# First batch's local probabilities turned on TensorE into strips of 64 keys

## The chip, the cores and the metric

One program runs on one core of a Trainium2 chip. The metric is the device time of one execution in microseconds; the kernel before takes 929.92 us (median of 3 runs, 927.62 to 931.52). Engines are named as in the profile: PE is TensorE, DVE VectorE, ACT ScalarE, POOL GpSimd, SP SyncE, which issues most DMAs.

## The reference

Attention over 8 batches, 8 heads, 576 positions, 64 dimensions, then a gated feed-forward network (FFN) over the 4608 tokens. Heads 0 to 3 see the last 32 positions ("local"), heads 4 to 7 every 32nd position ("strided"):

```python
rel = pos[:, None] - pos[None, :]
mask_local = (rel >= 0) & (rel < 32)
mask_strided = (rel >= 0) & (pos[None, :] % 32 == pos[:, None] % 32)
scores = np.where(masks, scale * q @ k.T, -1e9)
attn = softmax(scores)
x = (attn @ v).transpose(0, 2, 1, 3).reshape(4608, 512)
h = x @ w_in                      # 512 to 2048
g = h * clip(h + 3, 0, 6) / 6
out = g @ w_out                   # 2048 to 512
```

All data are fp32.

## The kernel before

**Work.** Heads go in pairs; a pair gives one chunk c of x, 128 features (two heads by 64) by 576 tokens. Chunks 0 and 1 are local, 2 and 3 strided. The first batch takes them in the order 0, 2, 1, 3 (`TURNS`). The FFN takes 512 tokens of a batch at a time, and the 64 left over of each batch are gathered and done four batches together. The FFN's operands are split into a high and a low fp32r part, so that each product is three matmuls: first product `ph` (lines 692 to 694, four chunks c for each of 16 blocks `fc` of the hidden dimension), gate (704, 708, 716, 721), second product `acc` (650 to 652). The weights come as raw fp32 by DMA (260) and are split on the chip, each part of 128x512 by two ACT activations (268, 272), a DVE join (276), a copy on ACT or POOL (282, 284) and a subtraction on POOL (288).

**A pair** (`pair`). q and k are loaded and turned so that the feature dimension is on partitions; in the first batch PE does this by products with the identity (441) and ACT or DVE copy the result out of PSUM (455, 457). Scores (526) go into two PSUM banks, one a head. For a local pair the queries stand in 6 blocks of 96, and each strip of 32 queries sees a window of 64 keys; so the probabilities e of a head are 96 partitions by 6 x 64. Mask, maximum, subtraction, exponential, sum, reciprocal and norm follow (542 to 565) on DVE, POOL and ACT. For the product with V the keys must be on partitions. `turn` (579) does this on DVE by transposes of 32x32 blocks: 6 instructions a head for a local pair (587), 4 for a strided one (584). `values` (590) multiplies V by the turned probabilities: for local pairs `window_products` (348), 7 products a head over windows of 128 keys, which `load_windows` (339) has loaded; for strided pairs the loop at 598. `keep_x` (359) moves the result into the FFN's operands, the high part by ACT (373), the low part by DVE (376).

**Order.** No loop order is written down. Each step is an `op` with engine, estimated cost, reads, writes and a due time, and `Plan.emit` is a list scheduler: again and again it takes the engine whose next operation can start first by its estimates, at equal times the one due first, and so fixes the order of every engine's instructions before anything runs. An `op` whose engine is a dictionary goes to the engine that can start first. DMA is modelled as one server: a load ends `after` us behind the later of its own start plus `FETCH` and the end of the load before it. `Slot` operations take a PSUM bank among several and give it back. Where the plan leaves PE idle for over `IDLE` us in the first 100 us, it puts in fillers (`idle`, 781), products of the identity with itself, one for each `IDLE` us of the planned gap; they end when the second bank of the first product is in use. An fp32 product is two matmul instructions, each with a weight load, so a filler is two records in the trace.

The lines at which this matters:

```python
if e == "PE" and t < WARM and t - free[e] > IDLE:
    for i in range(int((t - free[e]) / IDLE)):
        order.append((free[e] + i * IDLE, len(order), None, e))
...
if after:
    end = dma = max(t + FETCH, dma) + after
```

Of the kernel before, what the change touches and what calls it, by code (L numbers as in the profile page):

```python
# [10 lines left out]
F32 = mybir.dt.float32  # L11
# [19 lines left out]
TURNS = ((0, 2, 1, 3), (2, 0, 3, 1)) + ((0, 2, 1, 3),) * 6  # L31
AHEAD = 27.0
OPEN = 6.0
HIENG = {"ACT": 0.63, "POOL": 1.2}

# [6 lines left out]
HOP = 0.12  # L42

WARM = 100.0
IDLE = 0.22
FETCH = 2.2


class Plan:
# [29 lines left out]
    def emit(self, idle):  # L79
# [7 lines left out]
        free = dict.fromkeys(ready, 0.0)  # L87
        avail = [o[9] for o in ops]
        slots = {}
        mode, dma = "", 0.0  # L90

        def admit(n):
            for e in ops[n][0]:
# [69 lines left out]
def attention_ffn(ctx: ExitStack, tc, q, k, v, w_in, w_out, out):  # L163
# [80 lines left out]
    def wkey(w, g, i):  # L244
        return ("w", w, g, i)

    def weight_part(k, w, g, i):
# [39 lines left out]
            t = tiles[key]  # L287
            nc.gpsimd.tensor_tensor(out=t[:, 1], in0=tiles[fkey].bitcast(F32), in1=t[:, 0].bitcast(F32), op=ALU.subtract)  # L288

        op("SP", 0.53, load, writes=[key], due=-49 + 0.01 * k if k < 6 else -2 + 0.1 * k if k < 16 else due - 20.0, early=7.0 if k < 16 else due - 30.0, after=1.6 if k < 16 else 1.25)  # L290
        op("ACT", 0.68, high, reads=[key], writes=[fkey], due=due - 5, room=LATE + 1.0)
        op("ACT", 0.68, low, writes=[key], due=due - 5)
        op("DVE", 0.95, join, reads=[key], writes=[fkey], due=due - 3)
        op(HIENG, 0, hi, reads=[fkey], writes=[key], due=due - 2)
        op("POOL", 1.4, lo, reads=[fkey, key], writes=[key + ("lo",), key], due=due - 1)


    nn = [0]
# [11 lines left out]
    def either(us):  # L310
        return {"POOL": us, "DVE": us}
# [27 lines left out]
    def load_windows(t, b, h0):  # L339

        nc.sync.dma_start(t[PAD:, 0], v[b, h0:h0 + 2, 0:QB].rearrange("h p d -> p h d"))
# [43 lines left out]
    def pair(g):  # L385
# [33 lines left out]
        for x in "qk":  # L419
# [6 lines left out]
            if early:  # L426
# [9 lines left out]
                def tr(x=x, nkey=nkey, tb=tb, rows=rows, ni=ni):  # L436
                    ps = [psum(tb[h], f"{x}p{nm}{h}") for h in range(2)]
                    half = ni // 2
                    for i in range(ni):
                        for j in range(2):  # L440
                            nc.tensor.matmul(ps[i // half][D * j:D * j + D, i % half * rows:i % half * rows + rows],
                                             tiles[nkey][:rows, j, D * i:D * i + D], tiles["ident",][:rows, :rows],
                                             start=True, stop=True)

                def evac(e, x=x, tb=tb, h=0):
                    ps, to = tiles[tb[h].key][:, :S // 2], qk_of(x)
# [8 lines left out]
                        nc.scalar.copy(to, ps)  # L455
                    else:
                        nc.vector.tensor_copy(to, ps)
                op("ACT" if g < 2 and x == "k" else "SP", 0.55, load, writes=[nkey], due=-60 + 2 * g + (x == "k") - 900 * (g < 2 and x == "k"), after=1.05)
# [20 lines left out]
        vkey = wkey("i", NQ - 1, c) if early else ("vt",) if loc else ("vs",)  # L479
        if early:  # L480
            def clear(e):
                t = new(wp, vkey, [P, 6, 2, D] if loc else [P, 2, 8, D], F32, f"v{nm}")
                on(e).memset(t[:PAD, 0] if loc else t, 0.0)
            op(either(0.15 if loc else 0.9), 0, clear, writes=[vkey], due=due - 31)

        def load_v():
            if loc:
# [5 lines left out]
        op("SP", 1.6 if loc else 2.1, load_v, writes=[vkey], due=(-52, -48.8, -51, -48.5)[g] if early else due - 30, early=0 if early else due - 35, after=1.9)  # L493


        ekeys = [("el" if loc else "es", j) for j in range(2)]
        akeys = [("atl" if loc else "at", j) for j in range(2)]
        stkey = ("st", g % 2)
        nblk = NQB if loc else 8
        n = QB if loc else P  # L500
# [77 lines left out]
        for j in range(2):  # L578
            def turn(j=j):
                at, e = tiles[akeys[j]], e_whole(j)  # L580
                for a in range(n // PAD):
                    rows = slice(PAD * a, PAD * a + PAD)
                    if not loc:
                        nc.vector.transpose(at[rows, :, rows], e[rows])  # L584
                        continue
                    for h in range(2):
                        nc.vector.transpose(at[PAD * (a + h):PAD * (a + h) + PAD, :, rows], e[rows, :, PAD * h:PAD * h + PAD])  # L587
            op("DVE", 6 * 0.37 if loc else 4 * 0.435, turn, reads=[ekeys[j]], writes=[akeys[j]], due=due - 2 + j)

        def values():  # L590
            ps = [psum(vb[h], f"pv{nm}{h}") for h in range(2)]
            vt, ats = tiles[vkey], [tiles[x] for x in akeys]
            if loc:
                window_products(*ps, vt, ats)
                return
            for i in range(8):
                for j in range(2):
                    nc.tensor.matmul(ps[i // 4][D * j:D * j + D, i % 4 * P:i % 4 * P + 4 * NPOS], vt[:, j, i],  # L598
                                     ats[j][:, i].rearrange("p (a m) -> p a m", a=4)[:, :, :NPOS], start=True, stop=True)
        op("PE", 1.25 * slow, values, reads=[*akeys, vkey], writes=[*vb, *xk, lk], take=vb, due=due - 1001,  # L600
           room=0.0 if early else ROOM, mode="v")
        if loc:
# [146 lines left out]
    def first_tiles():  # L749
# [4 lines left out]
    op("POOL", 0.1, first_tiles, writes=["plain"], due=-30)  # L754
# [5 lines left out]
    for j in range(2):  # L760
        zero(("at", j), ap, [P, 8, P], F32, 1.1, 8 + j, f"atstr{j}")

    def values_loc():
        nc.gpsimd.memset(new(ap, ("vt",), [P, NQB, 2, D], F32, "vloc")[:PAD, 0], 0.0)
    op("POOL", 0.1, values_loc, writes=[("vt",)], due=20)
    zero(("vs",), ap, [P, 2, 8, D], F32, 1.1, 21, "vstr")
    for g in range(NPAIR):
        pair(g)
    for n, part in enumerate(parts):
        weight_part(n, *part)  # L770
    for t in seq:
# [9 lines left out]
    def idle():  # L781

        if ("ph", 1) in tiles:
            return
        if warm[0] is None:
            warm[0] = pp.tile([P, TOK], F32, tag="ph_1", name="idle")
        nc.tensor.matmul(warm[0][:, :P], tiles["ident",], tiles["ident",], start=True, stop=True)

    with tc.manual_schedule():
        plan.emit(idle)  # L790
# [30 lines left out]
```

## Time and profile before

The runs took 927.62, 929.92 and 931.52 us. The profiled execution took 930.79 us, its span (first to last instruction) is 929.0 us.

| engine | busy us | share of the span | instructions |
|---|---|---|---|
| PE | 907.4 | 98% | 8138 |
| PEld | 748.3 | 81% | 8138 |
| DVE | 433.2 | 47% | 972 |
| ACT | 320.7 | 35% | 608 |
| POOL | 329.2 | 35% | 360 |

PE is the matmul row, PEld the weight loads that overlap it. The mean granted TensorE clock is 0.99. The share of DMA time is high in the first 5% of the span and low behind it. In the timeline a row gives start, length, engine, line, operation, output and inputs, shape and count; in brackets stands the idle time of the engine ahead of the row and what ended it. "issue" means that nothing which the profile shows was waited for. A row that groups several instructions runs from the first start to the last end.

### The profile page before, as it was taken

The page shows a single profiled execution, that of the slowest core. Times are in us where ns is not written, and L with a number is a line of the kernel's source. Part 1 is how long each engine was busy: PE and PEld are TensorE (multiplying, and loading weights), DVE is VectorE, ACT ScalarE, POOL GpSimd, SP SyncE. Part 2 cuts the span into 40 slices and gives each one's busy share as a digit, 9 for nine tenths or more (in the row PEclk, how much of TensorE's full clock was granted, in tenths as well). Part 3 has the DMA queues.
Part 4 walks back from the last instruction along what each step waited for, and adds up shares of the span by engine and source line. Part 5 has one row for each costly group of instructions (what it writes and reads, how often), then busy time and mean ns, then how long its engine had stood idle before and what let it go on. Part 6 is the DMA issues. An engine that isn't in the chain of part 4 may idle for free.

```text
span 929.0 us, 19543 instructions
## 1 busy us (share of the span) xinstructions
PE 907.4 (98%) x8138; PEld 748.3 (81%) x8138; DVE 433.2 (47%) x972; ACT 320.7 (35%) x608; POOL 329.2 (35%) x360
## 2 busy tenths in 40 slices
PE   7889989999999999999999999999999999999997
PEld 7768867888888888988888888888888888888896
DVE  4888876554545424334245454555454541111111
ACT  2557665323233223332123222322233222322332
POOL 3568866232323223323223232323232322222221
PEclk9979999999999999999999999999999999999999
DMA  8948413222232203111222212222223200100101
GB/s 241 304 84 286 135 27 83 62 40 43 39 88 40 43 1 84 27 40 39 40 43 63 54 24 44 71 44 40 43 39 88 39 2 1 45 1 1 44 3 24
DMA packets 171209, 57.11 MB, mean 61 GB/s; under 512 B 158768, under 2 KB 159536, under 8 KB 171120
## 3 DMA queue, kind: packets, MB, share of 16 engines
q1 hardware_dynamic: 170756, 55.27, 24.3%
q8 instruction: 64, 1.05, 0.5%
q10 hardware_dynamic: 364, 0.59, 0.2%
q14 instruction: 25, 0.20, 0.1%
HBM read 46.40 MB, written 9.44 MB: 60 GB/s over the span
## 4 chain that ended last, share of the span: by engine, by line
PE 84%; issue 0%; POOLq 0%; DVE 0%
PE acc L650 12%; PE ph L692 12%; PE acc L652 11%; PE acc L651 11%; PE ph L693 11%; PE ph L694 11%; PE ps L526 3%; PE pv L356 2%; PE phl L692 2%; PE phl L693 2%; PE phl L694 2%; PE accl L652 2%; PE accl L650 2%; PE accl L651 2%; PE pv L598 1%
## 5 line engine op out<-in xcount | busy, mean ns | idle before, releaser
L721 POOL TENSOR_TENSOR gl<-u,gh 128x512 fp32r<-128x512 f32 x128 | 166.5, 1301 | 431.4 <-ACT gh L716 320.2
L692 PE MATMUL ph<-x,wi 128*128 128x512 f32 x512 | 205.6, 402 | 4.8 <-DVE u L708 2.1
L704 ACT ACTIVATE u<-ph,three 128x512 f32<-128x512 f32 x128 | 88.2, 689 | 340.7 <-PE ph L694 340.4
L693 PE MATMUL ph<-x,wi 128*128 128x512 f32 x512 | 201.9, 394 | 1.9 <-DVE left L376 1.0
L708 DVE SCALAR_TENSOR_TENSOR u<-u,ph 128x512 f32<-128x512 f32 x128 | 88.0, 688 | 246.8 <-ACT u L704 240.9
L694 PE MATMUL ph<-x,wi 128*128 128x512 f32 x512 | 201.6, 394 | 1.2 <-POOL wi L288 1.2
L650 PE MATMUL acc<-wo,gh 128*128 128x512 f32 x512 | 202.4, 395 | 0.0
L652 PE MATMUL acc<-wo,gl 128*128 128x512 f32 x512 | 199.5, 390 | 0.0
L651 PE MATMUL acc<-wo,gh 128*128 128x512 f32 x512 | 199.4, 389 | 0.0
L692 PEld LDWEIGHTS ph<-x,wi 128*128 128x128 f32 x512 | 97.0, 190 | 27.6 <-DVE u L708 2.5
L694 PEld LDWEIGHTS ph<-x,wi 128*128 128x128 f32 x512 | 97.4, 190 | 22.9 <-POOL wi L288 2.4
L693 PEld LDWEIGHTS ph<-x,wi 128*128 128x128 f32 x512 | 97.3, 190 | 21.8 <-DVE x L376 2.0
L716 ACT CAST gh<-u 128x512 fp32r<-128x512 f32 x128 | 79.5, 621 | 102.2 <-DVE u L708 101.3
L650 PEld LDWEIGHTS acc<-wo,gh 128*128 128x128 f32 x512 | 96.2, 188 | 20.9 <-DVE u L708 0.3
L652 PEld LDWEIGHTS acc<-wo,gl 128*128 128x128 f32 x512 | 96.1, 188 | 20.9 <-POOL gl L721 0.2
L651 PEld LDWEIGHTS acc<-wo,gh 128*128 128x128 f32 x512 | 96.2, 188 | 19.3
L587 DVE STREAM_TRANSPOSE atloc<-e 32x192 f32<-32x192 f32 x192 | 70.6, 368 | 14.4 <-POOL e L565 9.6
L552 POOL TENSOR_TENSOR e<-e,st 96x384 f32<-96x384 f32 (+1 forms) x64 | 42.5, 680 | 60.7 <-DVE st L548 60.7
L584 DVE STREAM_TRANSPOSE atstr<-e 32x256 f32<-32x256 f32 x128 | 55.6, 434 | 15.3 <-POOL e L565 13.9
L376 DVE TENSOR_TENSOR x<-pv,x 128x256 fp32r<-128x256 f32 (+1 forms) x48 | 31.5, 656 | 51.8 <-ACT left L373 28.2
L565 POOL TENSOR_TENSOR e<-e,st 96x384 f32<-96x384 f32 (+1 forms) x64 | 41.2, 658 | 20.3 <-DVE st L561 20.3
L721 POOL TENSOR_TENSOR gll<-ul,ghl 128x256 fp32r<-128x256 f32 x31 | 22.9, 739 | 65.5 <-ACT ghl L716 57.7
(96 smaller groups left out, 935.6 us busy)
## 6 DMA issues: line engine op xcount, KB each, us to landing
rawi<-in_moe_w_in_dram SPq DMA_DIRECT2D x16, 512.0 KB
rawo<-in_moe_w_out_dram SPq DMA_DIRECT2D x16, 512.0 KB
out_dram<-ob SPq DMA_DIRECT2D x32, 256.0 KB
qn<-in_q_dram SPq DMA_DIRECT2D x112, 72.0 KB
kn<-in_k_dram SPq DMA_DIRECT2D x112, 72.0 KB
vloc<-in_v_dram SPq DMA_DIRECT2D x28, 160.0 KB
vstr<-in_v_dram SPq DMA_DIRECT2D x56, 72.0 KB
qn<-in_q_dram SPq DMA_DIRECT2D x4, 288.0 KB
```

Of the source, the lines that this page charges most:

```text
L584: nc.vector.transpose(at[rows, :, rows], e[rows])
L587: nc.vector.transpose(at[PAD * (a + h):PAD * (a + h) + PAD, :, rows], e[rows, :, PAD * h:PAD * h + PAD])
L650: nc.tensor.matmul(acc, gh, woh, start=fc == 0, stop=False)
L651: nc.tensor.matmul(acc, gh, wol, start=False, stop=False)
L652: nc.tensor.matmul(acc, gl, woh, start=False, stop=end)
L692: nc.tensor.matmul(ph, wih, xh, start=n_ == 0, stop=False)
L693: nc.tensor.matmul(ph, wih, xl, start=False, stop=False)
L694: nc.tensor.matmul(ph, wil, xh, start=False, stop=n_ == NCC - 1)
L704: nc.scalar.activation(u, tiles[pk][:, :n], AF.Relu, bias=three)
L708: nc.vector.scalar_tensor_tensor(out=u, in0=u, scalar=6.0, in1=tiles[pk][:, :n], op0=ALU.min, op1=ALU.mult)
L716: nc.scalar.copy(g, tiles[uk][:, :n])
L721: eng.tensor_tensor(out=g, in0=tiles[uk][:, :n], in1=tiles[gk[0]][:, :n].bitcast(F32), op=ALU.subtract)
```

## The change

In the first batch's two local pairs the probabilities are no longer turned on DVE. For each head six products with the identity on PE (`upright`, 64 keys by 96 queries each) put them into one PSUM bank: the first three blocks of queries on partitions 0 to 63, the other three on 64 to 127. ACT copies the bank, 128 x 288, into a new tile `at64`. V is loaded in windows of 64 keys, one for each strip of 32 queries, strips 0 to 8 on partitions 0 to 63 and 9 to 17 on 64 to 127, into a tile for each head of its own. The values are 18 products a head, 32 columns each, over 64 partitions; the result stands in the two PSUM banks as 288 queries each, so that three instead of two pieces are kept as x.

With it go numbers of the planner: the modelled start of the first DMA (`FIRST`), costs of the weight split and of loads, the order of the V loads, and fillers of 384 instead of 128 columns, planned at 0.64 instead of 0.22 us. The V buffer of later local pairs is cleared behind the first batch, since `at64` lies in its place.

```diff
-HIENG = {"ACT": 0.63, "POOL": 1.2}
+HIENG = {"ACT": 0.63, "POOL": 0.7}
-IDLE = 0.22
+IDLE = 0.64
+FIRST = 3.4
-        mode, dma = "", 0.0
+        mode, dma = "", FIRST
...
-        op("SP", 0.53, load, writes=[key], due=-49 + 0.01 * k if k < 6 else ...
+        op("SP", 0.53, load, writes=[key], due=-49 + 0.01 * k if k < 4 else -48.4 + 0.01 * k if k < 6 else ...
-        op("DVE", 0.95, join, reads=[key], writes=[fkey], due=due - 3)
+        op("DVE", 1.05, join, reads=[key], writes=[fkey], due=due - 3)
-        op("POOL", 1.4, lo, reads=[fkey, key], writes=[key + ("lo",), key], due=due - 1)
+        op("POOL", 1.3, lo, reads=[fkey, key], writes=[key + ("lo",), key], due=due - 1)
...
+    def upright(ps, half, c0, data):
+        rows = data.shape[0]
+        nc.tensor.matmul(ps[D * half:D * half + D, c0:c0 + rows], data, tiles["ident",][:rows, :rows], start=True, stop=True)
+
+    def load_half_windows(ts, b, h0):
+        for j in range(2):
+            src = v[b, h0 + j]
+            nc.sync.dma_start(ts[j][PAD:D, 0], src[:PAD])
+            for p0, w0, base in ((0, 1, src[:D]), (D, 0, src[8 * PAD:8 * PAD + D])):
+                win = bass.AP(tensor=base.tensor, offset=base.offset, ap=[[D, D], [PAD * D, 9 - w0], [1, D]])
+                nc.sync.dma_start(ts[j][p0:p0 + D, w0:], win)
+
+    def half_window_products(pss, vs, at):
+        for u in range(9):
+            for half in range(2):
+                rows = slice(D * half, D * half + D)
+                for j in range(2):
+                    nc.tensor.matmul(pss[half][D * j:D * j + D, PAD * u:PAD * u + PAD], vs[j][rows, u],
+                                     at[rows, j, PAD * u:PAD * u + PAD], start=True, stop=True)
...
-                op("ACT" if g < 2 and x == "k" else "SP", 0.55, load, ..., after=1.05)
+                op("ACT" if g < 2 and x == "k" else "SP", 0.55, load, ..., after=1.15)
...
+        first = b == 0 and loc
+        if first:
+            vkeys = [wkey("i", NQ - 1, j) if c else ("n", j) for j in range(2)]
-        op("SP", 1.6 if loc else 2.1, load_v, writes=[vkey], due=(-52, -48.8, -51, -48.5)[g] if early else due - 30, ..., after=1.9)
+        op("SP", 2.6 if first else 1.6 if loc else 2.1, load_v, writes=vkeys, due=(-52, -48.8, -48.7, -48.5)[g] if early else due - 30, ..., after=3.2 if first else 2.0)
...
+            tb = slot(early)
+            def stand(j=j, tb=tb):
+                ps = psum(tb, f"pe{nm}{j}")
+                for i in range(NQB):
+                    upright(ps, i // 3, i % 3 * QB, e_whole(j)[:, i, :w])
+            def copy(j=j, tb=tb):
+                nc.scalar.copy(tiles["at64"][:, j], tiles[tb.key][:, :3 * QB])
+            op("PE", 0.7 * slow, stand, reads=[("ident",), ekeys[j]], writes=[tb], take=tb, due=due - 1002 + j, mode="s")
+            op("ACT", 0.45, copy, reads=[tb], writes=[akeys[j]], give=tb, due=due - 2 + j)
...
+            if first:
+                half_window_products(ps, [tiles[x] for x in vkeys], tiles["at64"])
+                return
...
+        if first:
+            half = S // 2
+            keep_x(nm, b, c, [(vb[0], lambda ps: ps[:, :half], lambda x: x[:, :half], half, False),
+                              (vb[1], lambda ps: ps[:, :TOK - half], lambda x: x[:, half:], TOK - half, False),
+                              (vb[1], lambda ps: ps[:, TOK - half:half], lambda x: x, LEFT, True)], due)
...
-        nc.tensor.matmul(warm[0][:, :P], tiles["ident",], tiles["ident",], start=True, stop=True)
+        nc.tensor.matmul(warm[0][:, :3 * P], tiles["ident",], tiles["ident",].unsqueeze(1).to_broadcast([P, 3, P]), start=True, stop=True)
```

More of the change, by code (lines that the diff above doesn't have):

```diff
@@ L440, in tr @@
                         for j in range(2):
-                            nc.tensor.matmul(ps[i // half][D * j:D * j + D, i % half * rows:i % half * rows + rows],
-                                             tiles[nkey][:rows, j, D * i:D * i + D], tiles["ident",][:rows, :rows],
-                                             start=True, stop=True)
+                            upright(ps[i // half], j, i % half * rows, tiles[nkey][:rows, j, D * i:D * i + D])
                 def evac(e, x=x, tb=tb, h=0):
@@ L457, in evac @@
                         nc.vector.tensor_copy(to, ps)
-                op("ACT" if g < 2 and x == "k" else "SP", 0.55, load, writes=[nkey], due=-60 + 2 * g + (x == "k") - 900 * (g < 2 and x == "k"), after=1.05)
+                op("ACT" if g < 2 and x == "k" else "SP", 0.55, load, writes=[nkey], due=-60 + 2 * g + (x == "k") - 900 * (g < 2 and x == "k"), after=1.15)
                 op("PE", 0.13 * ni * slow, tr, reads=[("ident",), nkey, "plain"], writes=tb, take=tb, due=due - 1020, mode="s")
@@ L476, in pair, with clear @@
             op("DVE", 0.8 if loc else 1.25, tr, reads=[nkey, "plain"], writes=[tkey[x]], due=due - 18, early=max(due - AHEAD, T0 + OPEN), room=LATE)
-        vkey = wkey("i", NQ - 1, c) if early else ("vt",) if loc else ("vs",)
-        if early:
+        first = b == 0 and loc
+        vkeys = [("vt",) if loc else ("vs",)]
+        if first:
+            vkeys = [wkey("i", NQ - 1, j) if c else ("n", j) for j in range(2)]
             def clear(e):
-                t = new(wp, vkey, [P, 6, 2, D] if loc else [P, 2, 8, D], F32, f"v{nm}")
-                on(e).memset(t[:PAD, 0] if loc else t, 0.0)
-            op(either(0.15 if loc else 0.9), 0, clear, writes=[vkey], due=due - 31)
+                for j, x in enumerate(vkeys):
+                    t = new(wp if c else ap, x, [P, 9, D], F32, f"v{nm}{j}")
+                    on(e).memset(t[:PAD, 0], 0.0)
+            op(either(0.2), 0, clear, writes=vkeys, due=due - 31)
+        elif b == 0:
+            vkeys = [wkey("i", NQ - 1, c)]
+            def clear(e):
+                t = new(wp, vkeys[0], [P, 2, 8, D], F32, f"v{nm}")
+                on(e).memset(t, 0.0)
+            op(either(0.9), 0, clear, writes=vkeys, due=due - 31)
+        vkey = vkeys[0]
         def load_v():
+            if first:
+                load_half_windows([tiles[x] for x in vkeys], b, h0)
+                return
             if loc:
@@ L492, in load_v @@
                 nc.sync.dma_start(tiles[vkey][PAD * a:PAD * a + NPOS].rearrange("p j t d -> p j (t d)"), rows[a])
-        op("SP", 1.6 if loc else 2.1, load_v, writes=[vkey], due=(-52, -48.8, -51, -48.5)[g] if early else due - 30, early=0 if early else due - 35, after=1.9)
+        op("SP", 2.6 if first else 1.6 if loc else 2.1, load_v, writes=vkeys, due=(-52, -48.8, -48.7, -48.5)[g] if early else due - 30, early=0 if early else due - 35, after=3.2 if first else 2.0)
         ekeys = [("el" if loc else "es", j) for j in range(2)]
-        akeys = [("atl" if loc else "at", j) for j in range(2)]
+        akeys = [("at64" if first else "atl" if loc else "at", j) for j in range(2)]
         stkey = ("st", g % 2)
@@ L587, in turn @@
                         nc.vector.transpose(at[PAD * (a + h):PAD * (a + h) + PAD, :, rows], e[rows, :, PAD * h:PAD * h + PAD])
-            op("DVE", 6 * 0.37 if loc else 4 * 0.435, turn, reads=[ekeys[j]], writes=[akeys[j]], due=due - 2 + j)
+            if not first:
+                op("DVE", 6 * 0.37 if loc else 4 * 0.435, turn, reads=[ekeys[j]], writes=[akeys[j]], due=due - 2 + j)
+                continue
+            tb = slot(early)
[7 more added lines that the diff above has]
+            op("ACT", 0.45, copy, reads=[tb], writes=[akeys[j]], give=tb, due=due - 2 + j)
         def values():
             ps = [psum(vb[h], f"pv{nm}{h}") for h in range(2)]
+            if first:
+                half_window_products(ps, [tiles[x] for x in vkeys], tiles["at64"])
+                return
             vt, ats = tiles[vkey], [tiles[x] for x in akeys]
@@ L599, in values @@
                                      ats[j][:, i].rearrange("p (a m) -> p a m", a=4)[:, :, :NPOS], start=True, stop=True)
-        op("PE", 1.25 * slow, values, reads=[*akeys, vkey], writes=[*vb, *xk, lk], take=vb, due=due - 1001,
+        op("PE", 1.25 * slow, values, reads=[*akeys, *vkeys], writes=[*vb, *xk, lk], take=vb, due=due - 1001,
            room=0.0 if early else ROOM, mode="v")
-        if loc:
+        if first:
+            half = S // 2
+            keep_x(nm, b, c, [(vb[0], lambda ps: ps[:, :half], lambda x: x[:, :half], half, False),
+                              (vb[1], lambda ps: ps[:, :TOK - half], lambda x: x[:, half:], TOK - half, False),
+                              (vb[1], lambda ps: ps[:, TOK - half:half], lambda x: x, LEFT, True)], due)
+        elif loc:
             keep_x(nm, b, c, [(vb[0], lambda ps: ps, lambda x: x, TOK, False),
@@ L753, in first_tiles @@
         nc.gpsimd.memset(tiles["qplain"][:, 2 * S:], 0.0)
-    op("POOL", 0.1, first_tiles, writes=["plain"], due=-30)
+        tiles["at64"] = ap.tile([P, 2, 3 * QB], F32, tag="vt", name="at64")
+    op("POOL", 0.1, first_tiles, writes=["plain", ("at64", 0), ("at64", 1)], due=-30)
     for j in range(2):
@@ L761, in attention_ffn @@
         zero(("at", j), ap, [P, 8, P], F32, 1.1, 8 + j, f"atstr{j}")
-    def values_loc():
-        nc.gpsimd.memset(new(ap, ("vt",), [P, NQB, 2, D], F32, "vloc")[:PAD, 0], 0.0)
-    op("POOL", 0.1, values_loc, writes=[("vt",)], due=20)
     zero(("vs",), ap, [P, 2, 8, D], F32, 1.1, 21, "vstr")
@@ L768, in attention_ffn, with values_loc @@
         pair(g)
+    def values_loc():
+        nc.gpsimd.memset(new(ap, ("vt",), [P, NQB, 2, D], F32, "vloc")[:PAD, 0], 0.0)
+    op("POOL", 0.1, values_loc, writes=[("vt",), ("at64", 0), ("at64", 1)], due=20)
     for n, part in enumerate(parts):
```

2 lines of the change are left out of this document (1 added, 1 removed).

## The prediction

> **What bounds the kernel now.** I read the page first, then the table by stages, then PE's order of time. PE is the bound nearly everywhere:
>
> ```profile
> span 929.0 us, 19543 instructions
> ```
> ```profile
> 80.00:120.00 40.00, 40.00 (x365) 32.46 (x365) 33.47 (x63) 28.57 (x54) 32.82 (x32) 1.00 0.57 178
> 120.00:160.00 40.00, 36.39 (x324) 27.98 (x321) 26.85 (x58) 22.34 (x41) 28.65 (x26) 1.00 0.24 45
> 160.00:200.00 40.00, 40.00 (x414) 32.50 (x413) 23.49 (x56) 13.95 (x27) 12.52 (x14) 1.00 0.34 77
> ```
>
> Columns: stage, length, then busy time of PE, PEld, DVE, ACT and POOL, then granted clock, DMA share, GB/s. From 80 us on PE is full but for 3.6 us near 135. Nothing in the steady batches is touched by the change except the planner's costs, so what can be won or lost lies before about 140 us. There PE runs like this:
>
> ```profile
> 1.36 5.77 PE L787 MATMUL idle<-ident 128*128 128x128 f32 x30 [1.36 <-POOL ident masks.py:199]
> 7.06 1.21 PE L441 MATMUL qp<-ident,qn 96*64 96x96 f32 x24
> ...
> 15.98 1.43 PE L441 MATMUL qp<-ident,qn 96*64 96x96 f32 x16 [3.33 <-issue]
> ...
> 21.72 0.59 PE L526 MATMUL ps<-kplain,qplain 64*32 64x18 f32 x47 [0.51 <-issue]
> ...
> 27.74 3.73 PE L787 MATMUL idle<-ident 128*128 128x128 f32 x32 [0.96 <-issue]
> 31.40 1.28 PE L356 MATMUL pv<-atloc,v 128*64 128x96 f32 x28
> ...
> 36.32 0.47 PE L692 MATMUL ph<-x,wi 128*128 128x512 f32 x1
> ...
> 42.57 0.77 PE L526 MATMUL ps<-kt,qt 64*32 64x18 f32 x69 [2.16 <-issue]
> ...
> 55.22 1.22 PE L598 MATMUL pv<-atstr,v 128*64 128x72 f32 x32
> ...
> 60.68 0.80 PE L693 MATMUL ph<-x,wi 128*128 128x512 f32 x1 [0.96 <-DVE left L376]
> 61.83 1.46 PE L526 MATMUL ps<-kplain,qplain 64*32 64x18 f32 x128
> ...
> 67.23 0.46 PE L650 MATMUL acc<-wo,gh 128*128 128x512 f32 x1
> ```
>
> The first batch needs its four chunks of x in the order c=0, 2, 1, 3 (0 and 1 local, 2 and 3 strided). The FFN begins at 36.32 but starves until the values of c=3 (55.22) have become x, and the second product begins only at 67.23. The engine that feeds it is DVE:
>
> ```profile
> 23.85 2.28 DVE L587 STREAM_TRANSPOSE atloc<-e 32x192 f32<-32x192 f32 x6
> 26.70 2.23 DVE L587 STREAM_TRANSPOSE atloc<-e 32x192 f32<-32x192 f32 x6
> 31.12 0.64 DVE L276 SCALAR_TENSOR_TENSOR fi<-fi,rawi 128x512 int32<-128x512 int32 x1
> 41.33 2.28 DVE L587 STREAM_TRANSPOSE atloc<-e 32x192 f32<-32x192 f32 x6 [1.50 <-POOL e L565]
> 47.05 2.23 DVE L587 STREAM_TRANSPOSE atloc<-e 32x192 f32<-32x192 f32 x6
> ```
> ```profile
> 0.00:12.66 12.66, 11.28 (x222) 10.80 (x222) 6.87 (x18) 3.95 (x6) 5.83 (x25) 1.00 0.81 208
> 21.25:26.85 5.60, 5.06 (x127) 4.68 (x127) 4.79 (x17) 2.55 (x7) 2.09 (x4) 1.00 1.05 375
> 26.85:40.45 13.60, 12.57 (x254) 11.29 (x253) 11.12 (x29) 7.76 (x14) 5.90 (x7) 1.00 1.00 351
> 40.45:62.00 21.55, 15.08 (x181) 10.34 (x189) 19.66 (x47) 8.67 (x22) 14.25 (x17) 0.81 0.37 78
> ```
>
> From 21.25 to 62 DVE works 35.6 of 40.8 us (4.79 + 11.12 + 19.66), more than any engine that does not merely fill time, and 9.0 us of that are the four turns of local probabilities that the change takes away.
>
> The same table shows a second limit. I cut it where PE stops for "issue". Between two stops lie 127 + 127 = 254 instructions of PE and PEld, or 254 + 253 = 507, twice that; the first stop is at 444. The instruction queue agrees:
>
> ```profile
> q8 instruction: 64, 1.05, 0.5%
> ```
>
> Its columns are packets, MB and share. 64 packets for 2 x 8138 PE instructions are 254 each. PE resumes at 15.98, 21.72 and 27.74: a block comes every 5.7 to 6.0 us while the DMA share stands at 1.0. So until about 44 us PE cannot run more than some 254 instructions in 5.9 us, whatever the data allow. The Trainium skill ("Runtime: NRT & Kernel Launch", Instruction fetch mechanics) calls the crossing of such a block mostly hidden. The four stops, 3.33 + 0.51 + 0.96 + 2.16 = 7.0 us, say otherwise here; by the page the fetch terms below would be nothing and the gain some 2 us larger.
>
> **The change part by part.**
>
> *DVE.* Four turns go, 2.28 + 2.23 + 2.28 + 2.23 = 9.0 us, half of it before c=2's work and half before c=3's.
>
> *PE, uprights.* Each head gets 6 products with the identity, two passes each: 12 records. The row at 7.06 has 24 records of the same shape in 1.21 us, so 0.6 us a head, 2.4 us in all.
>
> *PE, value products.* 18 a head, 36 a pair, 72 records instead of 28. No row has 32 columns on 64 rows by 64. The nearest, at 61.83, has 128 records of 18 columns in 1.46 us, 11.4 ns each: 0.8 us. The row at 31.40 (96 columns) gives 46 ns each: 3.3 us, the other end. I take 0.9 against 1.28 now, as the narrow row is nearer in columns and in rows. The Trainium skill ("TensorE: Matmul & The Clock Gate", Wait — 56ns, not 53.3ns?) states that starts never come closer than about 25 ns, which would make it an estimated 1.8 us; the row at 61.83 undercuts that by half, so the row decides.
>
> *ACT.* Four copies of 128x288 out of PSUM; the same shape took
>
> ```profile
> 10.31 0.40 ACT L455 COPY qplain<-qp 128x288 f32<-128x288 f32 x1 [0.32 <-PE qp L441]
> ```
>
> so 1.6 us. ACT is busy 16.4 of 35.2 us from 26.85 to 62 (7.76 + 8.67), so this is covered unless a copy queues behind another instruction; then it costs about 0.5 us, half the row of two at 20.93 below.
>
> *Fillers.* They are three times as wide and planned at 0.64 instead of 0.22, so the same planned gap takes a third of the instructions: 106 records become about 36. The first load is planned to land at 4.67 instead of 3.37 (FIRST 3.4 + 1.15 + 0.12 against 2.2 + 1.05 + 0.12), so PE starts with 7 wide fillers, the work of 21 old ones, instead of 15. The row at 1.36 (30 records, 15 fillers) and the one at 27.74 (16 in 3.73, 0.23 each) give 6 x 0.23 = 1.4 us more before the first transpose. That is covered by a wait behind it:
>
> ```profile
> 14.08 1.60 POOL L552 TENSOR_TENSOR e<-e,st 96x384 f32<-96x384 f32 x2 [6.94 <-DVE st L548]
> ```
> ```profile
> 20.93 0.95 ACT L555 ACTIVATE e<-e 96x384 f32<-96x384 f32 x2
> ```
>
> The exponential of c=0 could start once POOL is done (15.68) and starts 5.2 us later, because ACT's queue has c=1's copies before it and those wait for the transposes that the fetch stopped at 12.65. Without that cover the 1.4 us count in full; if the stop falls elsewhere, up to 5 us are won instead.
>
> *Fetch.* In instructions (two for each record): uprights +96, products +176, fillers -140, net +132, half a block, about 3 us. Up to the first FFN product only c=0's half is due (48 + 88 = 136 against -140): nothing. The half behind it, for c=1, falls after 40 us, where the table's DMA share drops to 0.37; I count 0, at most 3.
>
> *Loads.* Half windows read 1120 rows of 256 B a head, 573 KB a pair, against 368 KB (two of 160 and one of 48); 0.41 MB more at 351 GB/s is 1.2 us of saturated DMA. But c=1's V now goes behind the first four weight loads, which moves these forward by as much. SP and the queues behind: the next batch's first q and k wait for c=0's V tile and the local V buffer for c=1's product; by the rows
>
> ```profile
> 33.98 7.68 SPq L337 DMA_DIRECT2D qn<-in_q_dram  x4
> ...
> 63.27 0.55 SPq L341 DMA_DIRECT2D vloc<-in_v_dram  x1
> ```
>
> both issue later than those products run now (31.40) or will run, so nothing; held up, they would delay only loads of the next batch, whose scores run at 61.83.
>
> *Sum, by marks.* (1) c=0's values:
>
> ```profile
> 24.16 0.83 POOL L565 TENSOR_TENSOR e<-e,st 96x384 f32<-96x384 f32 x1
> ...
> 31.99 0.61 POOL L284 CAST wi<-fi 128x512 fp32r<-128x512 f32 x1
> 32.68 1.28 POOL L288 TENSOR_TENSOR wi<-fi,wi 128x512 fp32r<-128x512 f32 x1
> ...
> 55.74 2.03 POOL L284 CAST wo<-fo 128x512 fp32r<-128x512 f32 x2 [1.43 <-DVE fo L276]
> ```
>
> The second norm ends at 24.99; an upright (0.6), a copy (0.4) and hops put the products near 26.5 instead of 31.40. (2) The first weight is joined at 31.12 because DVE is still turning; 2 to 4 us earlier lets POOL end it near 31 instead of 33.96, and the FFN start near 33 instead of 36.32: the fetch, with edges at about 16.5 + 5.9 n (the first one half a microsecond later than now) and about as many instructions ahead as now, has its third edge behind the first stop at 34.2, so I take 33 to 34, or 30 if c=1's scores move behind it. (3) c=3's scores sit on the block edge that now resumes at 42.57; the fourth edge, 16.5 + 4 x 5.9, is at 40.1: 2 us earlier. (4) From there to 55.22 DVE carries c=1's second turn and a queue that has 9.0 us less: c=3's values near 47.5, some 7.5 us earlier. (5) x of c=3 and the second product follow, 67.23 becoming about 58.7: **8.5 us earlier**, the DVE time that went less what fetch keeps. (6) Then the first tile meets its weights:
>
> ```profile
> 133.02 0.50 PE L694 MATMUL ph<-x,wi 128*128 128x512 f32 x1 [0.63 <-POOL wi L288]
> ...
> 140.17 0.50 PE L692 MATMUL ph<-x,wi 128*128 128x512 f32 x1 [2.06 <-DVE u L708]
> ```
>
> The converters must be as much earlier. POOL's run of conversions starts at 55.74 waiting for DVE's join, so it moves with DVE, but not wholly: I take 1 us back. Net -7.5: span 921.5. The profiled execution took 930.79 against its span of 929.0 (1.8 around it) and 0.87 above the median 929.92; so 929.92 - 7.5 = **922.4**.
>
> **The rivals.**
>
> (a) *The clock stays up and more is won.* The half-clock stretches are
>
> ```profile
> 46.00:48.00 2.00, 2.00 (x5) 1.62 (x6) 1.65 (x7) 1.82 (x4) 0.93 (x3) 0.50 0.74 142
> ...
> 64.00:66.00 2.00, 2.00 (x7) 1.52 (x6) 1.22 (x4) 1.14 (x2) 1.56 (x3) 0.50 0.34 60
> ```
>
> about 7 us each from 43.3 and 60.7, of which half is lost. If x comes without the gaps ahead of them, up to 6 us more go: -13.5, 916.4. Against it: PE arrives earlier and still waits for c=3.
>
> (b) *The weights are the bound.* From 80 to 120 POOL works 32.8 of 40 us and DVE 33.5; if the conversions keep their place, an earlier start is waited away at 133 to 140 and at most 3 us remain: 927 to 930. For it: PE already waits for POOL there. Against: DVE's backlog is 9 us less, and the waits of ACT, whose output DVE and POOL take, say that the helpers are themselves paced by PE (in total 12.0 us from 56 to 140):
>
> ```profile
> ACT u L704 <- PE ph L694: 12.0, 10, 2.9
> ```
>
> (c) *Slower: the fetch.* The new costs reorder the head. If the planner keeps as many filler instructions and puts c=3's scores one to two blocks later, each block is 5.9 us, and a stop of over 3 us brings another half-clock stretch of 7 us (3 us lost): 5.9 + 5.9 + 3 - 8.5 = +6, 936. It decides if c=3's scores end after about 52 us instead of 43.3.
>
> **How the numbers follow.** Forecast (918 to 925) 0.48, (a) 0.15, (b) 0.24, (c) 0.13. A measurement of this kernel tells about 0.5% (4.6 us) from no change; below 925.3 lie the forecast and (a) less a little: faster 0.61, same 0.26, slower 0.13. Range 914 to 932: it holds the forecast, most of (a), all of (b).
>
> **What would show it.** No turns of DVE before the next batch; 48 upright records and 144 narrow ones at 10 to 15 ns; the first FFN product at 31 to 35; c=3's values at 45 to 50; the second product at 56 to 61; the waits near 135 grown by 1 us. It is wrong if "issue" stops take over 10 us in sum, if c=3's values come after 53, or if PE loses over 8 us between 100 and 150.

## The result and the profile after

The new kernel takes 927.09 us (median of 20 runs, 918.85 to 930.01) against 931.2 us of the kernel before measured with it (20 runs, 927.62 to 935.86). The ratio is 0.9935, 95% interval 0.9913 to 0.9958: about 6 us faster, a little beyond the half per cent that the prediction takes for the smallest change to be told. The times of the new kernel lie in two heaps: 14 of 20 from 925.76 to 930.01, 6 from 918.85 to 920.59. The profiled execution took 929.48 us, so it is one of the upper heap; a second profile (run after_again below) is of 925.05 us.

The page and the table by stages after (columns as before):

```profile
span 927.6 us, 19682 instructions
```
```profile
80.00:120.00 40.00, 39.62 (x410) 31.50 (x409) 32.78 (x65) 25.83 (x48) 34.08 (x33) 1.00 0.70 204
120.00:160.00 40.00, 39.86 (x357) 31.92 (x356) 31.56 (x67) 22.69 (x41) 29.58 (x29) 1.00 0.26 54
160.00:200.00 40.00, 39.05 (x409) 31.48 (x408) 19.06 (x42) 11.69 (x22) 9.87 (x11) 1.00 0.33 75
```

Between 80 and 200 us PE now idles 0.38 + 0.14 + 0.95 = 1.5 us, before 3.6. In the head, PE's order of time (after):

```profile
1.36 6.65 PE L847 MATMUL idle<-ident 128*128 128x384 f32 x14 [1.36 <-POOL ident masks.py:199]
...
17.27 0.91 PE L847 MATMUL idle<-ident 128*128 128x384 f32 x2 [3.09 <-issue]
...
25.21 0.43 PE L563 MATMUL ps<-kplain,qplain 64*32 64x18 f32 x27 [4.35 <-issue]
...
35.13 1.47 PE L369 MATMUL pv<-at,v 64*64 64x32 f32 x64
38.50 0.32 PE L369 MATMUL pv<-at,v 64*64 64x32 f32 x8 [1.90 <-issue]
...
43.67 1.54 PE L563 MATMUL ps<-kt,qt 64*32 64x18 f32 x128
...
46.63 1.43 PE L352 MATMUL pe<-ident,e 96*64 96x96 f32 x24
47.98 0.50 PE L750 MATMUL ph<-x,wi 128*128 128x512 f32 x1
...
49.58 1.25 PE L369 MATMUL pv<-at,v 64*64 64x32 f32 x72
...
57.08 1.22 PE L651 MATMUL pv<-atstr,v 128*64 128x72 f32 x32
...
64.30 0.47 PE L708 MATMUL acc<-wo,gh 128*128 128x512 f32 x1 [0.65 <-issue]
...
65.99 0.50 PE L710 MATMUL acc<-wo,gl 128*128 128x512 f32 x1 [0.99 <-POOL gl L779]
```

L352 are the products with the identity (`pe`: the uprights), L369 the 18 value products a head, L651 the strided ones, L750 the first product, L708 the second. The FFN starts at 47.98, 11.7 us *later* than before; c=3's values come at 57.08, 1.9 later; and yet the second product starts 2.9 us earlier, since the FFN, once begun, no longer starves: in both kernels 48 first products stand ahead of it. The wait of 0.65 us at 64.30 is named "issue", but PE's weight load for that product waited there for POOL's `wo` (1.0 us).

The same cut at the stops for issue:

```profile
0.00:14.20 14.20, 12.82 (x222) 9.40 (x222) 8.14 (x22) 3.89 (x6) 5.68 (x25) 1.00 0.82 199
14.20:20.90 6.70, 3.59 (x127) 2.73 (x128) 1.88 (x6) 1.89 (x5) 1.60 (x2) 0.84 0.94 284
20.90:36.65 15.75, 11.39 (x253) 9.65 (x253) 6.07 (x21) 4.86 (x12) 3.23 (x6) 0.52 0.81 255
```

444 instructions, 255, 506: the edges stand at the same counts as before the change. The last row has the other half of the story: the clock stands at 0.52. It fell to half at 18.8 us, behind the stop of 3.09 us and ahead of the one of 4.35 us, and stayed there for 17.1 us.

### The profile page after: what moved, and what is told of

It reads as the page before. It is cut to its first block, busy times and chain, and to the rows that moved or that the text cites. A ratio compares the mean times of both kernels' runs of the same rounds, so it can differ in the third digit from the quotient of the medians.

```text
span 927.6 us, 19682 instructions
## 1 busy us (share of the span) xinstructions
PE 907.6 (98%) x8196; PEld 743.4 (80%) x8196; DVE 426.5 (46%) x952; ACT 321.3 (35%) x607; POOL 331.4 (36%) x367
## 4 chain that ended last, share of the span: by engine, by line
PE 92%; issue 2%; POOL 2%; DVE 2%; DMA 1%; ACT 0%; SPq 0%; POOLq 0%; DVEq 0%
PE acc L708 13%; PE acc L710 12%; PE ph L750 12%; PE acc L709 12%; PE ph L752 12%; PE ph L751 12%; PE ps L563 4%; PE pv L651 2%; PE pv L380 2%; PE phl L750 2%; PE phl L752 2%; PE phl L751 2%; PE accl L710 2%; PE accl L708 2%; PE idle L847 2%
## 5 line engine op out<-in xcount | busy, mean ns | idle before, releaser
L766 DVE SCALAR_TENSOR_TENSOR u<-u,ph 128x512 f32<-128x512 f32 x128 | 87.9, 688 | 270.8 <-ACT u L762 269.8
L750 PE MATMUL ph<-x,wi 128*128 128x512 f32 x512 | 203.0, 397 | 1.5 <-DVE u L766 0.9
L708 PE MATMUL acc<-wo,gh 128*128 128x512 f32 x512 | 203.5, 397 | 0.6 <-issue 0.6
L752 PE MATMUL ph<-x,wi 128*128 128x512 f32 x512 | 199.7, 390 | 0.3 <-POOL wi L289 0.3
L751 PE MATMUL ph<-x,wi 128*128 128x512 f32 x512 | 199.5, 390 | 0.2 <-DVE x L400 0.2
L750 PEld LDWEIGHTS ph<-x,wi 128*128 128x128 f32 x512 | 96.1, 188 | 23.6 <-DVE u L766 1.9
L708 PEld LDWEIGHTS acc<-wo,gh 128*128 128x128 f32 x512 | 96.5, 188 | 22.0 <-POOL wo L285 1.0
L752 PEld LDWEIGHTS ph<-x,wi 128*128 128x128 f32 x512 | 96.1, 188 | 21.4 <-POOL wi L289 1.0
L751 PEld LDWEIGHTS ph<-x,wi 128*128 128x128 f32 x512 | 96.2, 188 | 19.3 <-DVE x L400 0.5
L624 DVE STREAM_TRANSPOSE atloc<-e 32x192 f32<-32x192 f32 x168 | 61.8, 368 | 6.9 <-POOL e L602 4.9
L400 DVE TENSOR_TENSOR x<-pv,x 128x256 fp32r<-128x256 f32 (+3 forms) x50 | 32.0, 640 | 48.9 <-ACT x L397 32.7
L592 ACT ACTIVATE e<-e 96x384 f32<-96x384 f32 (+1 forms) x64 | 26.8, 423 | 58.5 <-POOL e L589 57.7
```

Of the source, the lines that this page charges most:

```text
L708: nc.tensor.matmul(acc, gh, woh, start=fc == 0, stop=False)
L750: nc.tensor.matmul(ph, wih, xh, start=n_ == 0, stop=False)
L751: nc.tensor.matmul(ph, wih, xl, start=False, stop=False)
L752: nc.tensor.matmul(ph, wil, xh, start=False, stop=n_ == NCC - 1)
L766: nc.vector.scalar_tensor_tensor(out=u, in0=u, scalar=6.0, in1=tiles[pk][:, :n], op0=ALU.min, op1=ALU.mult)
```

## Experiments

In the table, "n" is the number of executions timed, "first" and "second" are the starts of the first and the second product in the one profiled execution; "stops" is PE's waiting for issue before 55 us; "half" the time at half clock before 200 us; "idle" PE's idle time from 80 to 200 us. All four vary between executions of a kernel, as the two rows of the new kernel (new and after_again) show; the ratio, to the kernel before in the same comparison, does not rest on them.

| kernel | ratio to before, 95% | n | first | second | stops | half | idle |
|---|---|---|---|---|---|---|---|
| before | 1 | 17 to 29 | 36.3 | 67.2 | 7.0 | 17.1 | 3.6 |
| new | 0.9935 (0.9913 to 0.9958) | 20 | 48.0 | 64.3 | 9.3 | 23.9 | 1.5 |
| after_again | 0.9940 (0.9911 to 0.9969) | 9 | 43.3 | 60.1 | 6.9 | 10.2 | 1.9 |
| turn_only | 0.9909 (0.9875 to 0.9943) | 7 | 42.5 | 55.8 | 6.5 | 6.8 | 2.5 |
| numbers_only | 1.0075 (1.0048 to 1.0103) | 12 | 38.6 | 68.6 | 7.4 | 23.9 | 5.2 |
| narrow_fillers | 0.9953 (0.9928 to 0.9977) | 10 | 46.5 | 65.2 | 9.5 | 13.7 | 1.9 |
| dve_turns_too | 1.0076 (1.0052 to 1.0100) | 12 | 44.0 | 69.9 | 7.0 | 17.1 | 4.5 |
| one_sixth | 0.9986 (0.9964 to 1.0008) | 12 | 48.8 | 62.1 | 6.9 | 13.7 | 7.0 |
| turn_wide | 0.9902 (0.9872 to 0.9933) | 6 | 44.6 | 58.1 | 4.1 | 20.5 | 2.5 |
| turn_costs | 0.9918 (0.9890 to 0.9947) | 6 | 43.7 | 59.5 | 6.0 | 13.7 | 0.8 |
| turn_order | 1.0029 (1.0009 to 1.0049) | 12 | 42.7 | 57.3 | 5.8 | 10.2 | 10.0 |
| order_early | 0.9979 (0.9954 to 1.0003) | 12 | 41.8 | 59.7 | 5.2 | 17.1 | 5.3 |
| after_old_order | 1.0003 (0.9985 to 1.0021) | 12 | 46.4 | 65.6 | 6.9 | 23.9 | 4.5 |
| late_weights | one execution, 939.19 us | 1 | 51.2 | 63.7 | 2.6 | 6.8 | 7.7 |

**The turn alone, and the planner's numbers alone.** turn_only is the new kernel with the old numbers and fillers; numbers_only is the kernel before with the new ones.

```diff
-HIENG = {"ACT": 0.63, "POOL": 0.7}
+HIENG = {"ACT": 0.63, "POOL": 1.2}
-IDLE = 0.64
+IDLE = 0.22
-        mode, dma = "", FIRST
+        mode, dma = "", 0.0
...
```

> The new kernel with the planner's old numbers (first DMA, costs, order of the loads) and the old narrow fillers: only the turn, its half windows of V and its products are new. Theory A (the time comes from DVE, which has four turns of 9.0 us less): most of the gain is here, ratio to the kernel before 0.991 to 0.996, no stall of 3 us near 135. Rival B (the time comes from the re-timed plan): ratio 0.998 to 1.004, the stall near 135 still about 3.5 us. Theory C (fetch: 136 more instructions ahead of the first FFN product and no narrower filler): first FFN product later than 48, ratio 1.000 to 1.008.

> The kernel before with the planner's new numbers, the new order of loads and the wide fillers; local probabilities still turned on DVE. Theory A: ratio 0.997 to 1.004, second product within 2 us of 67.2. Rival B: ratio 0.991 to 0.996 and the stall near 135 under 1 us. Theory C: some 70 filler records fewer, so the stops for issue before 45 us sum to under 6 us.

The turn is worth 0.9% (a hair more than theory A's range) and the numbers cost 0.75% by themselves, which no theory expected; together they give 0.65%, so the two effects don't add. Rival B falls. Theory C falls too: fewer fillers left the stops of numbers_only at 7.4 us (expected: under 6), and in turn_only, without the wide fillers, the fetch does not eat the gain. PE's order of time in turn_only has c=0's values at 21.84, c=3's at 48.23 and the second product at 55.77:

```profile
21.84 0.89 PE L368 MATMUL pv<-at,v 64*64 64x32 f32 x40
26.55 1.08 PE L368 MATMUL pv<-at,v 64*64 64x32 f32 x32 [3.82 <-issue]
...
48.23 1.22 PE L650 MATMUL pv<-atstr,v 128*64 128x72 f32 x32
...
55.77 0.47 PE L707 MATMUL acc<-wo,gh 128*128 128x512 f32 x1 [0.65 <-issue]
```

**Is it DVE's time?** dve_turns_too puts the four old turns back beside the new path, into a buffer that nobody reads. one_sixth goes the other way: the kernel before, with one transpose a head in place of six.

```diff
+            op("DVE", 6 * 0.37, spare_turn, reads=[ekeys[j]], writes=[("atl", j)], due=due - 2 + j)
             tb = slot(early)
```

> turn_only, and in addition the four old DVE turns into a buffer that nobody reads: the path of x stays on PE and ACT, DVE has its 9 us back. Theory A (DVE's time is what was won): 4 to 9 us slower than turn_only, ratio to the kernel before 0.995 to 1.003. Rival A2 (what was won is the shorter way of c=0's and c=1's x alone): ratio 0.988 to 0.994 as turn_only.

```diff
-                    for h in range(2):
+                    for h in range(2 if b else 1 - min(a, 1)):
...
-            op("DVE", 6 * 0.37 if loc else ...
+            op("DVE", (6 if b else 1) * 0.37 if loc else ...
```

> The kernel before, but of the six transposes that turn a head's local probabilities in the first batch only one is done (the rest of the turned tile stays zero, so part of the first batch's local attention is left out). DVE is 7.4 us lighter, PE and ACT get nothing new. Theory A (DVE's time before 62 us is what was won): ratio 0.986 to 0.994, second product at 58 to 62. Rival (what is won is the shape of the products or the plan): ratio 0.996 to 1.003.

The first answers for A, and more than expected: 9 us back on DVE cost 1.7% (1.0076 against 0.9909), some 15 us where 4 to 9 were expected. Rival A2 falls. But the kernel is now slower than the one before, which has the same turns on DVE, so not all of the 15 us is DVE's own time: the profiled execution had 10.2 us more at half clock than turn_only's, the plan is another one, and the spare turn holds the probabilities longer; no run separates these. PE's order of time there, with c=3's values behind DVE's queue:

```profile
52.14 0.47 PE L658 MATMUL pv<-atstr,v 128*64 128x72 f32 x2 [2.91 <-DVE atstr L620]
56.43 2.18 PE L658 MATMUL pv<-atstr,v 128*64 128x72 f32 x30 [3.82 <-DVE atstr L620]
```

The second, one_sixth, contradicts A as I had put it. The second product does come at 62.06, 5.2 us earlier, at the edge of what was expected of 7.4 us less DVE work (the two profiles of the new kernel differ by 4.2 in the same mark, so the size is rough), but the kernel is no faster. The stages behind the head show where it went (one_sixth):

```profile
80.00:120.00 40.00, 39.39 (x385) 31.41 (x382) 32.44 (x63) 26.20 (x49) 34.32 (x33) 1.00 0.64 187
120.00:160.00 40.00, 35.73 (x336) 27.69 (x335) 26.99 (x55) 22.33 (x40) 27.14 (x26) 1.00 0.20 37
160.00:200.00 40.00, 37.89 (x402) 30.15 (x401) 22.08 (x52) 12.02 (x24) 9.73 (x11) 1.00 0.37 85
```

PE idles 0.61 + 4.27 + 2.11 = 7.0 us, 3.4 more than before. So taking DVE's work away moves the head, and here most of what the head won was lost again behind it: 5.2 - 3.4 = 1.8 us would be left, and the ratio gives 1.3 (0.14%; its interval takes in no change). The ratio lies in the rival's range, so the plan may have its part in what is won or lost; the shape of the products has no run of its own.

**Which stage gives it back.** In the kernel before the largest part of the late idle time was a wait for DVE's gate at 140.17. DVE's order of time there (before):

```profile
134.22 4.58 DVE L587 STREAM_TRANSPOSE atloc<-e 32x192 f32<-32x192 f32 x12
138.83 0.69 DVE L276 SCALAR_TENSOR_TENSOR fo<-fo,rawo 128x512 int32<-128x512 int32 x1
139.44 1.28 DVE L708 SCALAR_TENSOR_TENSOR u<-u,ph 128x512 f32<-128x512 f32 x2
```

The gate stood behind twelve transposes of the *next* batch's turn in one piece, and a join. After the change the plan has other gates ahead and halves the piece (after, gates L766, turns L624):

```profile
138.39 0.69 DVE L766 SCALAR_TENSOR_TENSOR u<-u,ph 128x512 f32<-128x512 f32 x1 [0.57 <-ACT u L762]
...
139.69 2.24 DVE L624 STREAM_TRANSPOSE atloc<-e 32x192 f32<-32x192 f32 x6
...
143.37 2.28 DVE L624 STREAM_TRANSPOSE atloc<-e 32x192 f32<-32x192 f32 x6 [0.72 <-POOL e L602]
```

I take that for an accident of the list scheduler: but for the planner's costs and the later clearing of the V buffer, nothing in the change touches the second batch. How large such accidents are, turn_order shows, which is turn_only with only the new order of loads.

```diff
-due=-49 + 0.01 * k if k < 6 else ...
+due=-49 + 0.01 * k if k < 4 else -48.4 + 0.01 * k if k < 6 else ...
-due=(-52, -48.8, -51, -48.5)[g] if early else ...
+due=(-52, -48.8, -48.7, -48.5)[g] if early else ...
```

> turn_only with the new order of loads alone: the first four weight loads and strided V ahead of c=1's V. Theory E (with 512 KB weight loads queued from 15 us on, a fetch takes longer than behind V): stops for issue return between 12 and 24 us as in the new kernel, over 3 us in sum, ratio 0.993 to 0.998. Rival: order of loads does not matter, ratio and stops as turn_only (0.1 us of stops before 22 us).

It is slower than expected and for another reason. Its head is nearly as good as turn_only's (second product 57.3 against 55.8), and its stops are shorter in sum (5.8 against 6.5 us), so theory E's fetch is not the loss; 10.0 us are lost from 80 to 200 us. PE's waits there (turn_order):

```profile
PE ph L749 <- DVE u L765: 5.5, 3, 2.8
PE ph L751 <- POOL wi L288: 1.8, 2, 1.3
PE ph L749 <- POOL wi L284: 1.7, 1, 1.7
PE ps L562 <- DVE x L399: 1.1, 1, 1.1
```

Gates 5.5, weights 3.5. Besides, its clock fell to half for 6.8 us there, at 164.5 (mean clock 0.91 in the stage):

```profile
160.00:200.00 40.00, 37.20 (x388) 29.55 (x387) 20.68 (x48) 12.28 (x24) 10.20 (x12) 0.91 0.34 77
```

Against turn_only that makes 1.5 us of head, 7.5 us of idle time and, by estimate, half of the 6.8: 12.4 us of the 12.8 by which the spans differ. after_old_order, the reverse step on the new kernel (old order of loads, all else new), asked whether the new order costs everywhere.

> The new kernel with only the old order of the loads (both local pairs' V first). Theory E2 (the new order costs in every plan, since c=1's V and the fetches wait behind four weight loads): ratio 0.983 to 0.990. Rival (the loss of turn_order is that of one plan, in which the weights come late behind 80 us): ratio 0.991 to 0.998 as the new kernel.

It does not: there the old order is 0.6% slower (1.0003 against 0.9940), which neither theory E2 nor its rival expected. The sign of this edit depends on the plan in which it stands. order_early then made all weights in turn_order due 6 us earlier.

> turn_order (second product at 57.3 but 10.0 us of PE idle between 80 and 200 us) with all weight parts due 6 us earlier in the plan. Theory G (what the head wins is given back because the weights are split too late): PE idle from 80 to 200 us falls below 5 us, ratio 0.988 to 0.997. Rival (the idle time is that of the gate and of attention, not of the weights): 8 us or more stay, ratio 1.000 to 1.006.

The idle time fell to 5.3 us and the ratio from 1.0029 to 0.9979, both just short of the expected range; the waits for weights nearly went (0.6 us), those for the gate stayed (4.6). So the weights were part of it, and the gate in DVE's queue the rest.

**The fetch.** narrow_fillers is the new kernel with the old fillers; late_weights is turn_only with the first 16 weight loads held back.

> The new kernel with fillers of 128 columns planned at 0.22 again. Theory C (a block of 254 instructions takes some 6 us to fetch while DMA is saturated): about 56 more filler records, 112 instructions, before the first FFN product; the stops move to other instructions, and the first FFN product comes 1 to 4 us later; ratio to the kernel before 0.995 to 1.002. Rival (filler instructions cost nothing): the same times as the new kernel within 1 us.

> turn_only with the first 16 weight loads held back in the plan until 36 us. Theory C and E (fetch waits in the queues of saturated DMA engines): from 18 us until the weights start, fetch stops vanish (turn_only: 3.8 us at 22.7, 0.3 at 32.7, 2.4 at 38.4); they may return behind it. The time itself is 4 to 15 us worse than turn_only, since the weights come later. Rival (the stops are PE's own, 254 instructions in about 6 us): the stop near 22.7 stays at 3 us or more.

The DMA records of the traces show what the stops are. Instructions come in packets of 16 KiB, some 1 us each, and at every one of the 49 stops before 55 us in these 14 traces PE resumes 1.2 to 1.7 us after the end of such a packet. The long stops are those whose packet starts late: in the new kernel's first profile PE stands from 20.86, and the packet starts only at 22.59.

In narrow_fillers the stops move to other instructions, as expected: the first one now cuts c=0's scores, where the new kernel had it behind c=1's transposes.

```profile
16.34 0.30 PE L563 MATMUL ps<-kplain,qplain 64*32 64x64 f32 x4 [2.63 <-issue]
```

The first product is not later (46.5 against 48.0 and 43.3) and the time the same within the intervals, so half a block more of instructions (116) cost nothing that these runs can tell (its ratio, 0.9953, is just inside theory C's range and not to be told from the new kernel's). In late_weights, of which there is only the one execution, the stops shrink but don't vanish: the one at 22.7 in turn_only falls from 3.8 to 1.6 us. Its time is 14.9 us above turn_only's median, as expected of weights that come later. The stretch from 22 to 27 us, first turn_only, then late_weights:

```profile
22.00:27.00 5.00, 1.18 (x57) 1.07 (x59) 4.01 (x12) 1.32 (x2) 2.03 (x3) 0.89 1.02 390
```
```profile
22.00:27.00 5.00, 3.38 (x165) 3.01 (x162) 4.73 (x14) 1.19 (x4) 1.29 (x3) 1.00 0.30 82
```

At a DMA share of 1.02 PE issued 57 + 59 instructions, at 0.30 it issued 165 + 162. The packet for the stop near 22.7 started 3.9 us after PE had passed the edge before in turn_only, with DMA at 0.94 in between, and 1.5 us after it in late_weights, with DMA at 0.54. So the pace of the fetch is no fixed 6 us, as the prediction had it; it went with the load on DMA here. The size is rough, since the same stop differs by 3.1 us between the two executions of the new kernel below.

**The two heaps.** after_again is the new kernel, profiled once more.

> The new kernel unchanged, for a second profile: its 20 times fall in two heaps, 918.9 to 920.6 and 925.8 to 930.0. Theory D (a throttle window more or less): an execution of the lower heap has 7 to 14 us less at half clock before 70 us than the profiled one, which has 23.9, and shorter fetch stops at the same instructions. Rival: the heaps differ behind 70 us.

Its execution, 925.05 us, is between the heaps. The instructions are the same, the stops are not (after_again):

```profile
20.50 0.43 PE L563 MATMUL ps<-kplain,qplain 64*32 64x18 f32 x27 [2.73 <-issue]
...
33.26 0.32 PE L369 MATMUL pv<-at,v 64*64 64x32 f32 x8 [3.21 <-issue]
...
60.10 0.47 PE L708 MATMUL acc<-wo,gh 128*128 128x512 f32 x1 [0.65 <-issue]
```

The first stop (3.09 us at 14.2) is missing, since its packet started at 11.99 and not at 14.45; the second is 1.6 us shorter, the third 1.3 us longer, and two short ones come behind it (0.62 and 0.35). From 18.8 to 36 us the clock is higher; first the new kernel's first profile, then after_again:

```profile
18.80:36.00 17.20, 12.85 (x340) 10.87 (x339) 6.29 (x20) 6.02 (x14) 3.23 (x6) 0.50 0.82 269
```
```profile
18.80:36.00 17.20, 12.29 (x265) 9.68 (x265) 9.35 (x30) 7.04 (x18) 4.83 (x8) 0.73 0.91 297
```

13.7 us less at half clock and a second product 4.2 us earlier; the spans differ by 4.4. So these two executions differ in the head, as theory D has it. For the heaps themselves there is the mean granted clock of each execution: 0.993 to 1.000 in the 6 of the lower heap, 0.986 to 0.994 in the 14 of the upper (means 0.9955 and 0.9889). As the clock in the traces is either full or half, that is by estimate some 8 against 21 us at half clock, which agrees with theory D but does not say where in the run. No execution of the lower heap was profiled, and the nine times of after_again (921.26 to 930.32) show no gap like that between the heaps, so it is open whether there are two.

**Parts of the numbers.** turn_wide adds only the wide fillers to turn_only, turn_costs also the new costs of the weight split.

> turn_only with the wide fillers, planned at 0.64. Theory C (filler instructions take fetch blocks): faster than turn_only by 1 to 3 us, ratio 0.986 to 0.990, PE passes the first FFN product with some 60 records less. Rival: the wide fillers are part of what makes the new numbers slower, ratio 0.993 or more.

> turn_wide with the new costs of the weight split (copy on POOL 0.7, join 1.05, subtraction 1.3), without the new load order and the later first DMA. If these costs place the weights better: PE idle from 80 to 200 us under 2 us (turn_only and turn_wide: 2.5), ratio 0.984 to 0.989, the best so far. Rival: they are part of what makes the numbers alone slower: ratio 0.993 or more.

0.9902, 0.9918 and, without either, 0.9909: no difference that the intervals can tell, so neither gain that was expected came, although turn_costs has the least idle time behind the head (0.8 us). turn_wide suggests besides that half clock in the head need not cost half its length: it has 13.7 us more of it than turn_only, and its second product is 2.3 us later (one profile of each). All three have medians of 923.6 to 924.3, below the new kernel's 927.09 and 925.05; the intervals overlap with its own, so that they beat it is likely and not shown. What in the new numbers costs 0.75% by itself is left open.

## Why the prediction came out right, and which steps of it were wrong

The time lies in the range, the sign is right, and the size (7.5 us forecast, about 6 by the ratio, 4.1 by the medians) is near. That the gain comes from the turn was right too (turn_only). The steps did worse than their sum, and that the sum came near is in part luck: in the profiled execution the head won 2.9 us where 8.5 were forecast, and the stages behind it won 2.1 us where 1 was to be lost. By one of its own signs the prediction was wrong there: c=3's values came after 53, at 57.08 (52.93 in the second profile). Of the others, the turns went from DVE and the 48 and 144 records came as forecast; the first product was far too late, the second was behind 56 to 61 once (64.30) and within it once (60.10), and the waits near 135 shrank.

- **What bounds the head: DVE.** Right as far as it goes. Four turns put back cost 1.7%, more than their own time; five sixths of them taken out bring the second product 5.2 us forward, but the kernel hardly any.
- **Step 1, c=0's values near 26.5.** Wrong in the new kernel: 35.13 to 38.8. The stop of 4.35 us fell into the strided scores of c=2, and DVE's queue has their mask ahead of c=0's reciprocals and second sum (new kernel, the mask is L579):

```profile
25.82 0.31 DVE L579 TENSOR_TENSOR e<-ps,mtri 128x144 f32<-128x144 f32 x1 [4.50 <-PE ps L563]
26.04 0.18 DVE L598 RECIPROCAL st<-st 96x6 f32<-96x6 f32 x1
26.14 0.51 DVE L595 TENSOR_REDUCE st<-e 96x6 f32<-96x390 f32 x1
```

  All of it fell into the 17.1 us at half clock (18.8 to 35.9). I had found both mechanisms, the fetch and the half clock, in the trace and counted the fetch in average blocks, not at the place where the edge falls. In turn_only, where no stop to speak of came before 22.5 us, the first of these products ran at 21.84.
- **Step 2, FFN start near 33.** Wrong by 15 us: 47.98. The first product stands in PE's queue behind c=2's values, c=3's scores and c=1's uprights. I had kept the old order, though the planner writes a new one.
- **Steps 3 and 4, c=3's scores 2 us and values 7.5 us earlier.** Wrong: 43.67 against a resumption at 42.57, and 57.08 against 55.22.
- **Step 5, second product at 58.7.** It came at 64.30, and 60.10 in the second profile. The late start did not hurt, because the first products, which had been spread over stalls, now run in one stretch: from 47.98 until the last of them PE waits less than 1 us.
- **Step 6, 1 us given back to the weights.** Wrong sign: 2.1 us were won there. The row at 140.17 that I took for the weights' bound was the gate behind the next batch's turn. What rival (b) says, that an earlier start is waited away behind the head, is real all the same: one_sixth and turn_order are it, with 7.0 and 10.0 us of idle time, though the larger part of the waits is for the gate (4.1 and 5.5) and not for the weights.
- **The prices.** An upright pair took 1.43 us (forecast 1.2), 72 value records 1.25 us (forecast 0.9; between my two ends and 17 ns a record). The Trainium skill ("TensorE: Matmul & The Clock Gate", Wait — 56ns, not 53.3ns?) has 25 ns as the least from start to start; these records undercut it. The copies out of PSUM

```profile
L636 ACT COPY at<-pe x4: 393/398/399, 30.9 to 48.1; 128x288 f32<-128x288 f32 x4
```

(minimum, median and maximum in ns) took 0.40 us as forecast. The start-up fillers end at 8.01 instead of 7.13, 0.9 us later (forecast 1.4).

What remains as the account of the profiled pair of executions: second product 2.9 us earlier (-2.9); the next batch's first scores, 1.3 us of PE, now behind it instead of ahead (+1.3); less idle time from 80 to 200 us (-2.1); a wait for `gl` at 65.99 (+1.0); and 3.4 us of half clock from 66.6, half of it lost (+1.7). That is -1.0; the spans differ by -1.4. With after_again's own numbers (-7.1, +1.3, -1.7, and +1.1 for its waits for `gl`, no half clock) it is -6.4 against -5.8.

## What to carry to other kernels

Where a list scheduler writes the order, a gain in one stage counts only with the stages behind it: read the start of the next stage *and* the idle time after it, and test an edit of the planner's numbers in the plan in which it will stand, for the same new order of loads made one plan 0.6% faster and another 1.2% slower. A stretch of many small matmuls under saturated DMA can be stopped by instruction fetch (up to 4.35 us at an edge here); count the instructions to the next edge and ask whose result stands just behind it. A part that may be an accident (here the gate at 140) should be looked up in the waiting engine's own queue before it is put down to the engine's load.

## What was not expected of the hardware

PE's stops for issue before 55 us came only at the 444th matmul or weight load, or at multiples of some 254 behind it, whatever ran there and in every kernel of the study; their length for the same instruction of the same kernel was 3.1 us in one execution and nothing in another.

The Trainium skill ("TensorE: Matmul & The Clock Gate", HAM oscillation — how this bites in real kernels) says that idle gaps of PE of more than some 3.4 us bring the half clock. The traces here do not bear that out as a bound. Every half-clock stretch that ended within the run lasted 3.41 us or a multiple of it, and before 60 us each began during a stop of PE or at most 1.8 us behind one; but the stop could be far shorter than 3.4 us: 17.1 us at half clock began behind a stop of 3.09 us in the new kernel, 20.5 us around one of 2.29 us in turn_wide, and 17.1 us behind one of 1.22 us in after_old_order. So the "over 3 us" of the prediction's rival (c) is no bound either. The kernel before has one stretch that the prediction does not list, 3.4 us from 16.1, behind the stop of 3.33 us. What sets the length is left open.
